# A decode layer on one core: all loads in one byte ring in transfer order, K a group ahead of V, and another order of the matmuls

## The chip, the cores and the metric

One core of one Trainium2 chip. The time is the device time of one execution in microseconds, the median of three or more executions. The span, which the profile shows, is about 2 us shorter than the time. TensorE is PE, its weight loads PEld, VectorE DVE, ScalarE ACT, and SP is the engine that issues all the DMA loads here. A load lands when its last byte is in SBUF.

## The reference

A pre-norm decode step for a batch of 2, one token each: attention over a cached window of 2048 positions, 32 heads of 192, then a GEGLU feed-forward layer (FFN). Everything is bf16.

```python
h  = x + attention(layernorm(x))          # q = ln(x) @ wq   [640 x 6144]
                                          # K, V: 32 heads x 2 batches x 2048 x 192, read once
                                          # o @ wo           [6144 x 640]
h2 = h + (gelu(ln(h) @ w_gate) * (ln(h) @ w_up)) @ w_down   # 640 -> 1536 -> 640
```

K and V are 100 MB of the 122 MB that must be read, so the floor is set by the loads.

## The kernel before

The 64 (head, batch) items are worked in 16 groups of four. Each K tile (768 KB) is turned by 12 PE transposes into three PSUM banks, and copied to SBUF by DVE and ACT. Scores, softmax and PV (the softmax weights times V) follow per group. A small scheduler in the program derives the semaphore waits from tokens that each operation reads or writes. Every engine executes its own list in order, so the order in which operations are emitted is the order in which PE runs them.

```python
KS = 6; VS = 8; WQS = 2; WOS = 3          # slots: K ring, V ring, wq ring, wo ring; wd has its own tile

def load_k(n): ... kring[:, n % KS, :]    # each load waits for the readers of its slot
# gate and up weights reuse the K ring: kflat[:, 0:7680], kflat[:, 7680:15360]

def transposes(n):                        # 3 banks in turn, 4 fp32-pair transposes each
    for c in range(3):
        ...
        if c == 2 or (c == 1 and n % 4 == 1):
            act(... activation(out=ktr[...], in_=bank, func=Copy))   # 5 of 12 copies a group
        else:
            dve(... tensor_copy(out=ktr[...], in_=bank))             # 7 of 12

for g in range(NG):                       # PE's order
    for j in range(4):
        transposes(4 * g + j)
        if j == 0 and g > 0: scores(g - 1)
        if j == 1 and g > 1: o_columns(g - 2)
        if j == 1 and g > 0: softmax(g - 1)
        if j == 2: oproj(g - 2); e_columns(g - 1); q_rows(g + 1)     # (guards cut)
        if j == 3: q_stationary(g + 1)
    if g > 0: pv(g - 1)
# ... last group, then the FFN loads are issued: gate and up in 10 pieces of 384 KB, wd in 3 of 640 KB
# down: uT is stationary (2 columns), wd moves: 24 matmuls of 320 columns
```

Between scores of a group and its softmax, and between softmax and what follows it, PE always has 12 transposes of the next group to do.

## Time and profile before

| | before |
|---|---|
| time, median | 315.41 us (314.92 to 315.9) |
| span | 313.6 us |
| bytes loaded | 122.3 MB |
| PE busy | 77% |
| last V complete | 289.4 us |
| last FFN weight complete | 308.3 us |

From the page of the kernel before, two of the rows that cut the span into 40 slices of 7.84 us: DMA is the busy tenths of the 16 DMA engines.

```profile
DMA  7999999999999999999999999999999999996891
GB/s 252 416 416 418 395 402 420 415 411 406 414 414 419 399 417 414 419 408 406 414 417 416 401 412 416 418 410 403 414 416 418 412 416 418 415 411 260 280 386 41
```

The DMA engines are full from the first microseconds to slice 36; the drop to 260 and 280 GB/s is the end, where the FFN weights wait for the K ring. The same page's chain of waits (what released what, followed back from the last instruction) says the same:

```profile
DMA 43%; PE 40%; ACT 8%; DVE 7%; issue 1%; SPq 1%; POOL 0%; ACTq 0%; POOLq 0%; DVEq 0%
```

PE waits for K, not the other way round. A stretch of that chain in order of time (its longest pieces; start, duration, what), from a group in which no load was waited for:

```profile
64.55 1.43 PE ops L530 x64
65.99 1.46 PE tps L404 x12
67.45 1.48 PE sps L485 x23
68.93 1.04 PE tps L404 x8
70.05 1.94 ACT ktr L417 x2
```

PV (ops), 12 transposes (tps), scores (sps), transposes: 12 transposes take 1.46 us. From PV at 64.55 to the next PV at 77.77, in the same view, is 13.2 us for a group.

The end, from the timeline (start, duration, engine, line, operation):

```profile
286.10 0.33 SPq L600 DMA_DIRECT2D kring<-in_B_w_gate_dram  x1
...
290.37 0.33 SPq L602 DMA_DIRECT2D kring<-in_B_w_up_dram  x1
...
306.20 5.28 PE L654 MATMUL tps<-wd_sb,uT 128*2 128x320 bf16 x24 [0.63 <-DVE uT L291]
...
312.04 0.28 SPq L660 DMA_DIRECT2D out_dram<-orow  x1
```

The weights of the FFN are asked for at 286.1 and 290.4, the down matmuls take 5.3 us, and the store goes out at 312.0, 1.6 us before the end of the span.

### The profile page before, as it was taken

The page shows a single profiled execution, that of the slowest core. Times are in us where ns is not written, and L with a number is a line of the kernel's source. Part 1 is how long each engine was busy: PE and PEld are TensorE (multiplying, and loading weights), DVE is VectorE, ACT ScalarE, POOL GpSimd, SP SyncE. Part 2 cuts the span into 40 slices and gives each one's busy share as a digit, 9 for nine tenths or more (in the row PEclk, how much of TensorE's full clock was granted, in tenths as well). Part 3 has the DMA queues.
Part 4 walks back from the last instruction along what each step waited for, and adds up shares of the span by engine and source line. Part 5 has one row for each costly group of instructions (what it writes and reads, how often), then busy time and mean ns, then how long its engine had stood idle before and what let it go on. Part 6 is the DMA issues. An engine that isn't in the chain of part 4 may idle for free.

```text
span 313.6 us, 6955 instructions
## 1 busy us (share of the span) xinstructions
PE 241.1 (77%) x3081; PEld 193.2 (62%) x3081; DVE 123.2 (39%) x340; ACT 124.6 (40%) x151; POOL 3.2 (1%) x9
## 2 busy tenths in 40 slices
PE   0597059898886896979679893979759895979786
PEld 0385047787675675757458773766557784767663
DVE  8145023455444253434424541443423453443120
ACT  1256014557544244445415650544514553542100
POOL 4000000000000000000000000000000000000000
PEclk9999657999999587788958996996958997987767
DMA  7999999999999999999999999999999999996891
GB/s 252 416 416 418 395 402 420 415 411 406 414 414 419 399 417 414 419 408 406 414 417 416 401 412 416 418 410 403 414 416 418 412 416 418 415 411 260 280 386 41
DMA packets 29045, 122.74 MB, mean 391 GB/s; under 512 B 2644, under 2 KB 9304, under 8 KB 29016
## 3 DMA queue, kind: packets, MB, share of 16 engines
q1 hardware_dynamic: 29016, 122.31, 97.1%
q8 instruction: 24, 0.39, 0.5%
q14 instruction: 5, 0.04, 0.0%
HBM read 122.29 MB, written 0.00 MB: 390 GB/s over the span
## 4 chain that ended last, share of the span: by engine, by line
DMA 43%; PE 40%; ACT 8%; DVE 7%; issue 1%; SPq 1%; POOL 0%; ACTq 0%; POOLq 0%; DVEq 0%
DMA kring<-in_A_k_cache_dram 43%; PE tps L404 18%; PE ops L530 5%; PE sps L485 5%; PE m L430 4%; ACT ktr L417 3%; ACT qrow L435 3%; PE tps L654 2%; PE m L515 2%; DVE ktr L421 2%; PE m L455 1%; DVE ering L514 1%; ACT eexp L498 1%; PE m L544 1%; PE m L507 1%
## 5 line engine op out<-in xcount | busy, mean ns | idle before, releaser
L404 PE MATMUL tps<-identf,kring 128*128 128x128 f32 x768 | 118.4, 315 | 45.8 <-DMA kring<-in_A_k_cache_dram 45.4
L404 PEld LDWEIGHTS tps<-identf,kring 128*128 128x128 f32 x768 | 102.1, 163 | 62.7 <-issue 61.7
L417 ACT ACTIVATE ktr<-tps 128x1024 bf16<-128x1024 bf16 x80 | 80.2, 1023 | 114.1 <-PE tps L404 113.9
L421 DVE COPY ktr<-tps 128x1024 bf16<-128x1024 bf16 x112 | 74.4, 687 | 96.4 <-PE tps L404 96.1
L435 ACT ACTIVATE qrow<-m 2x1536 bf16<-2x1536 f32 x16 | 23.0, 1439 | 30.0 <-PE m L430 30.0
L530 PE MATMUL ops<-vring,ering 128*32 128x192 bf16 x1024 | 25.3, 254 | 0.0
L485 PE MATMUL sps<-ktr,rq 128*32 128x512 bf16 x384 | 24.9, 392 | 0.0
L530 PEld LDWEIGHTS ops<-vring,ering 128*32 128x32 bf16 x1024 | 21.5, 99 | 0.6 <-issue 0.3
L430 PE MATMUL m<-wqring,xnT 128*2 128x384 bf16 x80 | 21.1, 408 | 0.9 <-DVE xnT L291 0.9
L544 PEld LDWEIGHTS m<-sel,osb 128*128 128x128 f32 x96 | 18.0, 260 | 1.4 <-ACT osb L539 1.0
L490 DVE TENSOR_REDUCE mx<-sps 128x1 f32<-128x512 f32 x16 | 11.1, 692 | 19.3 <-PE sps L485 19.3
L544 PE MATMUL m<-sel,osb 128*128 128x2 f32 x96 | 17.9, 302 | 0.6 <-ACT osb L539 0.6
L485 PEld LDWEIGHTS sps<-ktr,rq 128*32 128x32 bf16 x384 | 9.0, 95 | 10.2 <-issue 2.5
L515 PE MATMUL m<-zrhs,hm 128*128 128x2 f32 x32 | 7.6, 306 | 9.7 <-DVE ering L514 9.7
L539 ACT ACTIVATE osb<-ops 128x384 f32<-128x384 f32 x16 | 7.9, 492 | 17.0 <-PE ops L530 17.0
L515 PEld LDWEIGHTS m<-zrhs,hm 128*128 128x128 f32 x32 | 6.2, 241 | 13.2 <-DVE ering L514 13.2
L498 ACT ACTIVATE eexp<-sps,nm 128x512 bf16<-128x512 f32 x16 | 11.1, 692 | 2.6 <-DVE nm L496 2.6
L430 PEld LDWEIGHTS m<-wqring,xnT 128*2 128x2 bf16 x80 | 6.3, 94 | 7.5 <-issue 4.2
L514 DVE COPY ering<-m 128x64 bf16<-128x64 bf16 x16 | 6.9, 432 | 9.2 <-PE m L507 9.2
L291 DVE TENSOR_TENSOR rq<-m,mask 128x24 bf16<-128x24 f32 x64 | 7.2, 175 | 6.8 <-PE m L455 5.6
L556 PEld LDWEIGHTS hps<-ot,woring 128*128 128x128 bf16 x240 | 9.3, 104 | 1.0 <-DVE ot L291 0.3
L455 PEld LDWEIGHTS m<-identb,qrow 2*128 2x128 bf16 x192 | 5.9, 93 | 6.3 <-ACT qrow L435 5.0
(82 smaller groups left out, 99.4 us busy)
## 6 DMA issues: line engine op xcount, KB each, us to landing
kring<-in_A_k_cache_dram SPq DMA_DIRECT2D x64, 768.0 KB, 17.9
vring<-in_A_v_cache_dram SPq DMA_DIRECT2D x64, 768.0 KB, 17.1
wqring<-in_A_wq_dram SPq DMA_DIRECT2D x8, 960.0 KB, 17.8
woring<-in_A_wo_dram SPq DMA_DIRECT2D x16, 480.0 KB, 18.6
kring<-in_B_w_gate_dram SPq DMA_DIRECT2D x5, 384.0 KB, 5.9
kring<-in_B_w_up_dram SPq DMA_DIRECT2D x5, 384.0 KB, 6.9
wd_sb<-in_B_w_down_dram SPq DMA_DIRECT2D x3, 640.0 KB, 11.0
xrow<-in_A_x_dram SPq DMA_DIRECT2D x1, 2.5 KB
```

The costliest lines, as they stand in the source:

```text
L404: ins = e.transpose(tps[bi][:, 128 * u:128 * (u + 1)], kv[:, off:off + 128], identf[:, :])
L417: act(lambda e, c=c, kslot=kslot, bv=bv: e.activation(out=ktr[:, kslot, c, :], in_=bv[:, 0:1024], func=ACT.Copy), W=[("kt", kslot, c)], X= ...
L421: dve(lambda e, c=c, kslot=kslot, bv=bv: e.tensor_copy(ktr[:, kslot, c, :], bv[:, 0:1024]), W=[("kt", kslot, c)], X=[("t", bi)])
L430: ins = e.matmul(m1[0:2, 128:512], lhsT=xnT[:, c, :], rhs=wqring[:, J % WQS, c, off:off + 384], start=(c == 0), stop=(c == NC5 - 1))
L435: act(lambda e: e.activation(out=qrow[0:2, :, 0:rep, :], in_=m1[0:2, 128:512].rearrange("p (h d) -> p h d", h=2).unsqueeze(2).to_broadcast ...
L485: ins = e.matmul(sps[32 * j:32 * (j + 1), :], lhsT=rq[:, g % 2, j, k, :], rhs=r, start=(k == 0), stop=(k == 5), tile_position=(0, 32 * j))
L490: dve(lambda e: e.tensor_reduce(out=mx[:, :], in_=sps[:, :], axis=AX.X, op=ALU.max), W=["mx"], X=["s"])
L498: act(lambda e: e.activation(out=eexp[:, :], in_=sps[:, :], func=ACT.Exp, bias=nm[:, 0:1], scale=1.0, accum_out=zr[:, 0:1]), R=["nm"], W=[ ...
L514: dve(lambda e: e.tensor_copy(dst, src), W=[("er", g % 2)], X=["m2"])
L515: pe(lambda e: e.matmul(m2[:, 8:10], lhsT=hm[:, :], rhs=zrhs[:, :], start=True, stop=True), R=["hm", "zrhs"], X=["m2"])
L530: ins = e.matmul(ops_[32 * r:32 * (r + 1), 192 * hh:192 * (hh + 1)], lhsT=ering[:, g % 2, col:col + 32], rhs=vring[:, n % VS, DH * t:DH * ...
L544: ins = e.matmul(m1[:, 32 + 2 * kk:34 + 2 * kk], lhsT=osb[:, kk:384:3], rhs=sel[:, :], start=True, stop=True)
```

## The change

The intent: one ring of 110,592 bytes per partition holds K, V, wq, wo and the FFN weights, in the order in which they are transferred, so that no ring can run dry while another has room, and the FFN weights queue directly behind the last V. The ring is kept account of in granules of 768 bytes (GRAN): a load waits for the readers of every granule that it covers, so two pieces that share a granule wait for each other. K runs a group ahead of V. q is made for four groups at a time from one 1.9 MB load. Down has wd stationary and 2 moving columns, so that little is left after the last load.

```diff
-KS = 6
-VS = 8
-WQS = 2
-WOS = 3
+GRAN = 768
+RING = 18 * 6144
@@ loads: a queue, issued as soon as every older load on those bytes has been read
+        def pump():
+            while queue: ...
+                toks = [("ring", x) for x in range(off // GRAN, (off + nbytes + GRAN - 1) // GRAN)]
+                P.op("sp", lambda e, v=v, src=src: e.dma_start(v, src), W=toks + [("sem", i % NSEM)], ...)
+        load_k(0)
         load_wq(0)
+        load_k(1)
+        for g in range(NG):
+            if g > 0 and g + 1 < NG:
+                if (g + 1) % 4 == 0:
+                    load_wq((g + 1) // 4)
+                load_k(g + 1)
+            load_v(g)
+            load_wo(g)
+        load_ffn()
@@ PE's order
         for g in range(NG):
+            if g + 1 < NG:
+                for j in range(4):
+                    transposes(4 * (g + 1) + j)
+                    if (g + 1) % 4 == 0:
+                        q_rows(g + 1 + j)
+                q_stationary(g + 1)
+            pv(g, 0)
+            if g + 1 < NG:
+                scores(g + 1)
+            pv(g, 1)
+            pv(g, 2)
+            if g + 1 < NG:
+                softmax(g + 1)
+            pv(g, 3)
+            o_columns(g)
+            if g + 1 < NG:
+                e_columns(g + 1)
+            oproj(g)
@@ weights with contiguous rows per partition, so columns are read with a stride
-    lhsT=woring[:, g % WOS, kk, 128 * n5:128 * (n5 + 1)]
+    lhsT=wo[:, kk, c:D:NC5]                       # stride 5
-    lhsT=wv[:, c, 128 * f:128 * (f + 1)]          # gate, up
+    lhsT=wv[:, c, f:F:NF]                         # stride 12
@@ down
-    ins = e.matmul(tps[bank][0:2, 0:320], lhsT=uT[:, f, :], rhs=wd_sb[:, f, 320 * bank:320 * (bank + 1)], ...)
+    ins = e.matmul(m2[:, 2 * c:2 * c + 2], lhsT=wd[:, f, c:D:NC5], rhs=uT[:, 4 * i + f, :], ...)
@@ output: straight from the 128 x 2 x 5 result, 256 pieces of 10 bytes, instead of 2 rows
@@ cut: names of tokens, constants built after the first layernorm, q rows repeated 2 instead of 4 times
```

## The prediction

> **What bounds the kernel now.** The span is 313.6 us (time 315.8: 2.2 us lie outside it). The slice table shows the DMA row at 9 from 8 us to 274 us, at 395 to 420 GB/s; 122.3 MB moved. The chain of waits is 43% K loads. The body is bound by loads; PE (77% busy) waits for them. What is not stream is the end: the last V is complete at about 289.5 us, the gate/up loads wait for the K ring (issued 286.1 and, because the first up piece shares ring slots with the first gate piece, only after that landed, 290.4), 288-292 us moves 110 GB/s, wd streams until 307.5, down takes 5.3 us (306.2-311.5), output 1.6 us.
>
> The trace's landing records: each load lands on 16 DMA engines (Trainium skill, "DMA: Bandwidth & Descriptors", section on why a DMA increments its semaphore by 16: they finish independently, only the full count counts). The trace agrees: the first-to-last spread grows from 0.4 us at the start to 5.4 us at 289 us, in jumps of about 1 us that coincide with 16 KB instruction-fetch packets (1.1 us each). The fast engines finish V at 284, the slow one at 289.5. That lag survives the change.
>
> **What the change does.** Steady state: only packet size. Median packets: 1536 B (wq) 66 ns, 3072 B 121 ns, 6144 B 238 ns; wq in 3072 B rows saves about 1.5 us over the run. The K/V order is off the bound; PE work per group (my estimate 15 us, from the chain's 13 to 15 us stretches plus serial softmax waits) stays below the 17.4 us of loads per group, so DMA should not starve. Late constants and q for 4 groups: off the path.
>
> End: with FFN loads queued behind the last wo, the slow engine completes wo15 at about 288.0 us; wg, wu (1.97 MB each) and wd0 follow without gap: +11 us, 299. PV, output projection, layernorm, gate, GELU (10.7 us before, 295.5-306.2, with 1.4 us of residual matmuls removed) hide behind them. Down becomes 60 short matmuls (28 ns apart for the same form at gate/up); only the last 20, 0.6 us, follow the last load, instead of 5.3 us.
>
> But the wd pieces are 5120 B in 768 B granules, so neighbours share a granule, and the built program makes wd1's issue wait for wd0's semaphore and wd2's for wd1's. Before shows such an isolated load: the first up piece, 393 KB, took 3.0 us from issue to landing; 655 KB thus about 3.7 us (estimate). wd2 lands near 306.3 instead of 302. Then matmuls, an add, a scattered output store: 2.7 us. Span 309.
>
> **Predicted: 311.0 us (-1.5%), 80% range 307.0 to 314.5. Faster by over 2%: 0.28; within 2%: 0.68; slower: 0.04.**
>
> **Right if:** DMA still about 415 GB/s; gate/up issued long before landing; wd1 and wd2 waiting for a load in the SP queue's waits (two dips in the last 10 us); under 3.5 us after wd2's landing.
>
> **Wrong if:** the wd waits cost under 1 us each (307); strided weight loads (every 5th or 12th bf16) are slow: stride 2 shows no penalty (92 ns), every third f32 takes 261 ns against 190 contiguous; at 100 ns apart, 317; PE falls behind after q for 4 groups and stalls the ring (+2 to 5); the slowest engine's fetch lag changes by some us.

## The result, and the profile after

| | before | after |
|---|---|---|
| time, median | 315.41 us | 325.52 us (323.86 to 327.21) |
| ratio | | 1.032 (1.026 to 1.038) |
| last V complete | 289.4 us | 289.0 us |
| last PV done | 295.5 us | 303.0 us |
| last FFN weight complete | 308.3 us | 309.5 us |

A ratio is the mean time of one kernel's fast runs over that of the other's in the same rounds, so it is not quite the ratio of the medians quoted.

The change made it 10 us slower. The slices of the page after (8.1 us each now; PEclk is the TensorE clock that the throttle granted, in tenths of full speed):

```profile
PEclk9997797979799786979799897979796898979555
DMA  7999999999999999999999999999999999998310
GB/s 274 416 416 414 419 417 416 410 409 419 413 391 329 422 413 419 411 412 414 414 386 413 418 414 417 407 418 414 413 368 419 419 414 415 414 427 371 104 66 0
```

The loads still run at 416 GB/s and nearly end with slice 37, three slices before the end; three dips (329, 386, 368) have appeared. And the chain of waits no longer holds a load:

```profile
PE 59%; ACT 24%; DVE 12%; issue 3%; POOL 0%; ACTq 0%; POOLq 0%
```

PE, fed by ACT and DVE, has become the bound. One whole group of that chain, in order of time (its longest pieces; it answers to the stretch shown of before):

```profile
260.60 0.70 DVE mx L521
261.33 0.24 DVE mrhs L316
261.61 0.40 PE m L525 x2
262.03 0.17 DVE nm L527
262.29 0.78 ACT eexp L529 x2
263.07 0.39 ACT osb L570
263.50 1.21 PE m L575 x6
264.71 0.26 PE m L538 x4
264.99 0.45 DVE ering L545
265.48 0.38 PE m L546 x2
265.86 0.58 PE hps L589 x15
266.45 3.92 PE tps L433 x20
270.39 1.95 ACT ktr L448 x2
272.39 0.67 PE tps L433 x4
273.08 1.03 ACT ktr L448
274.16 0.67 PE tps L433 x4
274.85 1.03 ACT ktr L448
276.02 1.56 PE sps L516 x24
277.60 0.70 DVE mx L521
```

In it mx is the maximum of each row of scores, m L525 and nm bring the rows of an item together, eexp is the exponential, osb and m L575 turn the attention output of the group before, m L538 and ering turn the exponentials, and hps is the output projection. From one maximum (mx) to the next is 17.0 us. The first 5.85 us are the softmax block: each step waits for the one before it on another engine, and PE has only PV matmuls (32, then 16) to do beside them. Then come the 48 transposes in one burst, 9.6 us to the start of the scores. The first 20 take 3.92 us, 196 ns each, against 122 ns before (1.46 us for 12). The rest alternate with ACT's copies, since three PSUM banks are all that the kernel gives them and every bank must be emptied first. Then scores, 1.6 us. In the three of the fifteen periods that make q for four, the period is 20.3 us instead of 17.0. The mean over groups 2 to 16 (fourteen periods) is 17.8 us, and the loads of a group take 17.4 (9.25 tiles' worth on average, with wo and wq, at 1.88 us a tile from landing to landing).

The end of the kernel, from the timeline:

```profile
309.14 3.72 PE L637 MATMUL sps<-hnT,ring 128*128 128x2 bf16 x60 [0.80 <-DVE hnT L320]
...
316.69 2.56 PE L660 MATMUL m<-uT,ring 128*128 128x2 bf16 x60 [0.28 <-DVE uT L320]
...
319.49 0.41 SPq L668 DMA_DIRECT2D out_dram<-yT  x1
```

All weights are there at 309.5, but gate has only started. The 10.2 us of span divide as follows. PV of the last group ends 7.5 us later (303.0 against 295.5). From there to gate it is 0.6 us shorter; gate to the GELU product 7.5 us instead of 3.9 (+3.6); from there to the issue of the store 2.9 instead of 5.9 (-3.0); issue of the store to the end 4.3 instead of 1.6 (+2.7).

### The profile page after: what moved, and what is told of

It reads as the page before. It is cut to its first block, busy times and chain, and to the rows that moved or that the text cites. A ratio compares the mean times of both kernels' runs of the same rounds, so it can differ in the third digit from the quotient of the medians.

```text
span 323.8 us, 6976 instructions
## 1 busy us (share of the span) xinstructions
PE 255.5 (79%) x3105; PEld 203.3 (63%) x3105; DVE 126.1 (39%) x340; ACT 112.8 (35%) x150; POOL 3.2 (1%) x9
## 4 chain that ended last, share of the span: by engine, by line
PE 59%; ACT 24%; DVE 12%; issue 3%; POOL 0%; ACTq 0%; POOLq 0%
PE tps L433 27%; ACT ktr L448 16%; PE sps L516 8%; PE m L575 6%; PE m L461 4%; ACT eexp L529 4%; DVE mx L521 3%; PE hps L589 3%; DVE ering L545 2%; PE m L546 2%; PE m L525 2%; ACT osb L570 2%; ACT qrow L466 2%; PE m L538 1%; DVE mrhs L316 1%
## 5 line engine op out<-in xcount | busy, mean ns | idle before, releaser
L433 PE MATMUL tps<-identf,ring 128*128 128x128 f32 x768 | 124.3, 326 | 11.8 <-ACT ktr L448 8.9
L433 PEld LDWEIGHTS tps<-identf,ring 128*128 128x128 f32 x768 | 109.2, 170 | 24.9 <-ACT ktr L448 17.8
L575 PE MATMUL m<-sel,osb 128*128 128x2 f32 x96 | 19.9, 324 | 16.1 <-ACT osb L570 16.1
L575 PEld LDWEIGHTS m<-sel,osb 128*128 128x128 f32 x96 | 18.6, 270 | 19.9 <-ACT osb L570 19.9
L561 PE MATMUL ops<-ring,ering 128*32 128x192 bf16 x1024 | 30.7, 253 | 0.0
L561 PEld LDWEIGHTS ops<-ring,ering 128*32 128x32 bf16 x1024 | 21.8, 98 | 3.8
L516 PEld LDWEIGHTS sps<-ktr,rq 128*32 128x32 bf16 x384 | 9.7, 97 | 16.5 <-DVE rq L320 8.6
L461 PE MATMUL m<-ring,xnT 128*2 128x384 bf16 x80 | 17.7, 357 | 2.7 <-ACT qrow L466 2.7
L466 ACT ACTIVATE qrow<-m 2x768 bf16<-2x768 f32 x16 | 12.6, 790 | 4.9 <-PE m L461 4.9
L461 PEld LDWEIGHTS m<-ring,xnT 128*2 128x2 bf16 x80 | 5.7, 87 | 11.4 <-ACT qrow L466 4.4
L589 PEld LDWEIGHTS hps<-ot,ring 128*128 128x128 bf16 x240 | 12.1, 134 | 0.3 <-DVE ot L320 0.3
L525 PEld LDWEIGHTS m<-mrhs,pm 128*128 128x128 f32 x32 | 4.8, 188 | 11.3 <-DVE mrhs L316 11.3
L589 PE MATMUL hps<-ot,ring 128*128 128x2 bf16 x240 | 11.6, 177 | 0.3 <-DVE ot L320 0.3
```

The lines of the kernel that those rows point to most:

```text
L433: ins = e.transpose(tps[bi][:, 128 * u:128 * (u + 1)], kv[:, off:off + 128], identf[:, :])
L461: ins = e.matmul(m1[0:2, 128:512], lhsT=xnT[:, c, :], rhs=wq[:, c, off:off + 384], start=(c == 0), stop=(c == NC5 - 1))
L466: act(lambda e: e.activation(out=qrow[0:2, g % QS, :, 0:rep, :], in_=m1[0:2, 128:512].rearrange("p (h d) -> p h d", h=2).unsqueeze(2).to_b ...
L516: ins = e.matmul(sps[32 * j:32 * (j + 1), :], lhsT=rq[:, g % 2, j, k, :], rhs=r, start=(k == 0), stop=(k == 5), tile_position=(0, 32 * j))
L561: ins = e.matmul(ops_[32 * r:32 * (r + 1), 192 * hh:192 * (hh + 1)], lhsT=ering[:, g % 2, col:col + 32], rhs=vv[:, DH * t:DH * (t + 1)], s ...
L575: ins = e.matmul(m1[:, 32 + 2 * kk:34 + 2 * kk], lhsT=osb[:, kk:384:3], rhs=sel[:, :], start=True, stop=True)
```

## The experiments

Theory A: the new PE order is the loss. Before, transposes lay between the dependent steps of the softmax; now the steps are waited for one after the other and the transposes come in a burst, so a group costs PE 17 us or more. Theory B: the ring is the loss. It frees in order and leaves gaps at its end, so loads come late (the dips). Two smaller causes are separate: the strided weight loads of the FFN, and the waits between wd pieces on which the prediction put 4.4 us.

### 1. The changed kernel with the PE order of before (e1_interleave)

```diff
-        (the order shown in the change)
+        for g in range(NG):
+            for j in range(4):
+                transposes(4 * g + j)
+                if g % 4 == 0 and g > 0: q_rows(g + j)      # g == 0: all four after j == 3
+                if j == 0 and g > 0: scores(g - 1)
+                if j == 1 and g > 1: o_columns(g - 2)
+                if j == 1 and g > 0: softmax(g - 1)
+                if j == 2: oproj(g - 2); e_columns(g - 1)   # guards cut
+                if j == 3: q_stationary(g)
+            if g > 0: pv(g - 1, 0..3)
+        # cut: the last group, as in the kernel before
```

> The changed kernel with the PE order of the kernel before (K transposes of one group between scores, softmax and projection of the last), loads and FFN as changed. Theory A (the serial PE order is the loss: a group takes PE 17.0 us, 20.3 with q, against 17.4 us of loads): the chain is led by loads again, the dips to 270-350 GB/s in the body go, PV of the last group ends before 293 us instead of 303, time 311 to 317. Rival B (the byte ring, with its in-order freeing and wrap gaps, starves the loads): the dips stay and the time stays above 320. Then, with PE on time, the two waits of wd pieces should show as dips near the end.

Measured: 314.75 us, ratio to before 0.997 (0.994 to 1.000). Of the three dips one small one is left (376 GB/s). Where no load is waited for, a group takes 12.0 us from maximum to maximum instead of 17.0, and the last wo is complete at 287.75 us (the prediction had 288.0). Theory B alone cannot stand: ring, loads and FFN are all those of the changed kernel, and 10.8 us are gone.

The chain of this run ends with what the prediction had expected of the changed kernel:

```profile
298.46 3.93 DMA ring<-in_B_w_down_dram
...
302.47 3.87 DMA ring<-in_B_w_down_dram
...
306.39 1.77 PE m L667 x40
```

Two wd loads, each issued only when the one before has landed, 3.95 us from landing to landing for 1.6 us worth of bytes. They had been estimated at 3.7. And one detail nobody had seen: 40 matmuls come after the last load, not 20, because readers of a shared granule wait for its last writer too.

### 2. The kernel before with the PE order of the change (e2_before_order)

The reverse: rings, loads and FFN of before, K transposed a group ahead, then the serial order. q_rows stays one group at a time.

```diff
+        k_group(0); q_stationary(0); scores(0); softmax(0); e_columns(0)   # k_group: transposes, K loads, q_rows
+        for g in range(NG):
+            k_group(g + 1); q_stationary(g + 1)                            # guards cut
+            pv(g, 0); scores(g + 1); pv(g, 1); pv(g, 2); softmax(g + 1); pv(g, 3)
+            o_columns(g); e_columns(g + 1); oproj(g)
```

> The kernel before (its own rings, loads and FFN) with only the PE order of the changed kernel, K a group ahead. Theory A: PE becomes the bound, group period 17.5 to 18.5 us, time 320 to 328. Rival B (the ring is the loss, the order harmless): within 1% of before, 313 to 318.

Measured: 337.29 us, ratio 1.068 (1.065 to 1.072). The order alone makes the old kernel 22 us slower. The direction is theory A's, the size is beyond what was expected: after the first, periods are 17.9 to 19.2 us, because in this kernel every group also has its own q rows, whose copy takes ACT 1.44 us (0.79 in the changed kernel, where rows are repeated half as often) inside the burst that already waits for ACT. The changed kernel's cheaper q copy is thus a gain that its order hides. What q for four groups is worth by itself, no run shows: the shorter copy comes from the halved repetition.

### 3. Gate and up read contiguously (e3_contig)

```diff
-                        ins = e.matmul(..., lhsT=wv[:, c, f:F:NF], ...)
+                        ins = e.matmul(..., lhsT=wv[:, c, 128 * f:128 * (f + 1)], ...)
-            wd = B_w_down.rearrange("(p f) n -> p f n", f=NF)
+            wd = B_w_down.rearrange("(f p) n -> p f n", p=128)
```

> The changed kernel with the gate and up weights read contiguously (wd loaded in 1280 B rows to match), the rest as changed. If the stride of 12 is what makes a gate matmul 62 ns instead of 28: gate and up take 1.7 to 1.9 us each instead of 3.7 and 3.6, and, since PE is last, the time falls by 3 to 4 us to about 322. If the half clock is the cause instead: no change, 325.

Measured: 319.7 us, 5.8 us under the changed kernel's 325.52 (different rounds; ratios to before 1.013 and 1.032). The timeline of this run:

```profile
307.52 1.76 PE L637 MATMUL sps<-hnT,ring 128*128 128x2 bf16 x60 [0.79 <-DVE hnT L320]
```

Gate (this line) and up (1.74 us) take half as long as in the changed kernel (3.72 and 3.69) at the same granted clock (0.50 in both kernels). So the stride costs 62 ns a weight load against 28 to 29. That is 3.6 us of the 6.3 between the two profiled runs. The rest: gate began 1.6 us earlier, and the store was 1.1 us shorter; neither is explained by the edit. Runs of the changed kernel differ by 3.4 us among themselves, so the first may be chance.

The Trainium skill's page "SBUF — State Buffer" (the cacheline note) says that accesses that leave the 16-byte line each time pay a penalty, without a number for weight loads. The traces agree for steps of 24 bytes and supply numbers: stride of 4 bytes, 30 ns (12 q columns in 0.36 us before, on 2 partitions only and at a granted clock of 1.00); at 0.50, 10 bytes, 43 ns (60 down matmuls in 2.56 us); 24 bytes, 62 ns; contiguous, 28 ns. The note's figure for how far one can stride for free, 8 bf16 elements, they do not bear out: the step of 10 bytes is 5 elements and already costs.

### 4. Granules of 256 bytes (e4_gran256)

```diff
-GRAN = 768
+GRAN = 256
```

> The changed kernel with ring granules of 256 B instead of 768 B, so that wd pieces share none and do not wait for each other. The prediction put 4.4 us on these waits. Theory A (PE is 10 us late at the end): wd lands some 4 to 7 us earlier and the time moves by less than 1 us (324 to 326). If the waits cost what was predicted: about 321.

Measured: 325.14 us, ratio 1.029 (1.024 to 1.034). wd is complete at 302.6 us instead of 309.5, seven microseconds earlier, and nothing moves: PE reaches down at 315.8. The waits on which the prediction built its arithmetic existed and were hidden.

### 5. One more copy on DVE (e6_evac)

```diff
-                if c == 2 or (c == 1 and n % 4 == 1):
+                if c == 2:
```

> The changed kernel with its serial PE order kept, and one of the five K copies that ACT does per group moved to DVE (4 on ACT, 8 on DVE). Theory A, where the burst of 48 transposes waits for ACT's copies: the group's period falls from 17.0 to about 16.0 us, below the 17.4 us of loads, the dips shrink and the time falls to 314 to 320. If ACT's copies are not what stretches the burst: 325, no change.

Measured: 324.0 us, ratio 1.027 (1.019 to 1.036), its runs overlapping those of the changed kernel. A miss. PE's wait for ACT before transposes falls from 8.9 to 3.6 us in all, but the periods without q, after the first, are 16.5 us in five groups and 17.2 to 17.4 in six. In the six, part of a stretch of half clock fell into the softmax block (mean grant there 0.74 to 0.78 instead of 1.00), which then took 6.2 to 6.3 us instead of 5.7. So there is a second brake, the clock. The last wo was complete at 287.8 us here, as early as in experiment 1, and PE was still late.

### 6. Useless matmuls that keep PE busy in the softmax block (e9_warm)

```diff
+        def warm(n):                       # n matmuls of 128 x 88 columns into unused columns of m1
+            ...
             softmax(g + 1)                 # warm(6) before it
             pv(g, 3)
+            warm(18)
             o_columns(g)                   # and warm(8) inside e_columns, before the sum
```

> The changed kernel, its order kept, with 32 useless matmuls of 88 columns per group put where PE waits in the softmax block (before the max matmul, before the output columns, before the sum matmul). If the half clock after that block is what stretches the transposes (196 ns instead of 122 for the first 20 of 48 in a group): they run at 122, the period falls from 17.0 to 15.3 to 16 us although PE does more, loads lead again and the time falls to 314 to 319. If the clock is only a symptom: the period stays at 17 or grows, 325 to 328.

Measured: 318.32 us, ratio 1.009 (1.007 to 1.012); 506 more matmuls and 7 us faster than the changed kernel. In the groups that took 15.6 or 15.7 us, the chain reads:

```profile
209.02 2.55 PE tps L433 x20
```

The first 20 transposes take 2.55 us instead of 3.92. Of the eleven periods without q after the first, three came down to 15.6 or 15.7, three are 16.8 to 16.9, and five stayed at 17.0. (The first is 15.8, but it was 15.1 in the changed kernel.) The granted clock tells them apart. First the changed kernel around the start of a burst, then this run around a burst that stayed slow (stretch, its length, PE busy and instructions, granted clock, DMA share, GB/s):

```profile
263.06:266.47 3.41, 2.44 (x29) 1.00 1.03 421
266.47:269.88 3.41, 3.41 (x18) 0.50 1.03 419
269.88:273.29 3.41, 2.95 (x24) 1.00 0.99 407
```

```profile
242.07:245.48 3.41, 3.37 (x41) 1.00 1.02 409
245.48:248.90 3.42, 3.42 (x19) 0.50 1.02 418
```

In the three fast groups the grant stays at 1.00 through the burst, in the other eight its first 4 us are granted 0.57 to 0.59. Program and order are the same in all of them, so the clock is a cause, not only a symptom, and it is worth 1.4 us a group. That idle PE in the block is what lowers it is not shown: here PE was busy for 3.37 of the 3.41 us before the grant fell, and why three groups escaped is open. The Trainium skill's "TensorE: Matmul & The Clock Gate" (Part 1) describes a clock that is half by default and full only after a stretch of PE activity; the traces here agree that it is either half or full and comes back after 3.41 us of transposes, but a busy PE was not enough to keep it.

### 7. Two of four tiles transposed inside the softmax block (e10_two_early)

```diff
                 for j in range(4):
-                    transposes(4 * (g + 1) + j)
+                    if g == 0 or j > 1: transposes(4 * (g + 1) + j)
             pv(g, 3)
+            transposes(4 * (g + 2))          # guards cut
             o_columns(g)
             e_columns(g + 1)
+            transposes(4 * (g + 2) + 1)
             oproj(g)
```

> The changed kernel with two of the four K tiles of the next group but one transposed inside the softmax block (before the output columns and before the output projection), the rest of the order, loads and FFN as changed. Theory A (waits of the softmax block plus a burst that waits for copies): the period falls to about 15.5 us, under the 17.4 of loads, time 313 to 317, close to the fully interleaved 314.75. If only the complete order of before helps: above 320.

Measured: 314.92 us, ratio 0.998 (0.995 to 1.000). Groups that wait for no load take 13.6 us. The chain leads from loads again (38% DMA, 27% of it K), and the transposes in the block run at 122 ns, with a grant of 1.00 through block and burst (249.93 to 260.70):

```profile
250.94 0.38 PE m L525 x2
...
251.77 1.46 PE tps L433 x12
253.23 0.94 PE m L575 x6
```

Compare the same place of the changed kernel: from L525 at 261.61 to L575 at 263.50 PE had only 16 PV matmuls. Two moves undo the loss in the body; the complete order of before is not needed.

### 8. The parts put together (e5b_inter_gran, e5_all, e8_rowout)

Experiment 1 with 256-byte granules:

> The PE order of before with 256 B granules: the two waits of wd pieces, hidden where PE was late, should now be worth what they cost in the interleaved run (3.9 us each for 1.6 us of transfer). wd2 complete at about 302 instead of 306.7, 20 matmuls behind it instead of 40, time 309.5 to 311.5 (4 to 5 us under the interleaved run's 314.75). If it stays at 314 or more, something else paces the end.

Measured: 309.87 us, ratio 0.980 (0.975 to 0.986), 4.9 us under experiment 1. With PE on time the same one-line edit that did nothing in experiment 4 is worth what its waits cost. Last wd complete at 301.5 us.

The same with gate and up contiguous:

> The same, and gate and up read contiguously. The strided reads end at about 301 us in the run without it, before wd2 lands (302), so they should be hidden: 0 to 1 us less, 309 to 311. A gain of 3 us or more would say that the FFN matmuls are still on the path.

Measured: 307.94 us, ratio 0.9745 (0.969 to 0.980). 1.9 us less, where at most 1 was expected. The timelines show the difference: without it down begins at 301.05, 0.5 us before the last load lands, and its 60 matmuls end at 303.6; with it 20 remain after the last load, and the store is issued 0.7 us earlier. The store itself takes 2.9 us instead of 4.5 to the end of the span. The two kernels with contiguous gate and up and this store have 2.9 and 3.2 us, the seven strided ones 4.3 to 4.7, with the same store; why is open.

The same with the output turned into two rows on PE, copied by DVE and ACT and stored in 1280-byte pieces:

> The same, and the output turned into 2 rows on PE and stored in 1280 B pieces, instead of 256 pieces of 10 B. The store took 4.3 us from issue to the end of the span in the changed kernel against 1.6 us before; five matmuls and a split copy add about 1.3 us. Net 1 to 1.7 us less than the run before it: 307.5 to 309.5.

Measured: 308.37 us, no gain. The store does take 1.6 us, but the way to it from the last landing is 3.2 us instead of 1.3: DVE's copy of 2 x 384 with a stride of 5 in the output took 1.21 us, where the contiguous 2 x 320 copy of the kernel before took 0.48. The Trainium skill's "DMA: Bandwidth & Descriptors" (Specifications) asks for 512 bytes or more per piece; the trace agrees that 10-byte pieces are slow (2.9 to 4.7 us against 1.6), but avoiding them costs as much here.

The version of e5_all beats both kernels: 2.5% under before (by the interval of the ratio, 2.0 to 3.1%), 5.4% under the changed one (307.94 against 325.52, medians of different rounds).

## Why the prediction was wrong

- **The step that failed:** "PE work per group (my estimate 15 us ...) stays below the 17.4 us of loads per group, so DMA should not starve." Measured: 17.0 us, 20.3 with q, 17.8 in the mean. The estimate added the serial waits to durations of an interleaved kernel. It left out that a burst of transposes on three banks waits for its copies, and that after the serial block the clock is at half for the first 3.4 us of the burst. The burst takes 9.6 us where four tiles take 5.8 at 1.46 each. Of these 3.8 us the clock is about 1.4 (an estimate: the full-clock groups of experiment 6 against the others), and the remaining 2.4 would be waits for copies, the last one before the scores included. Experiments 1, 2 and 7 show that the order is the cause, 6 that the clock has a share; 5 that ACT's copies alone are not enough.
- **What followed from it:** the estimate left 2.4 us of slack per group; there were -0.4. And 17.4 was too generous a yardstick, since at the first maximum the loads have already been running for some 30 us. Where they lead (experiment 1), first and last maximum are at 29.4 and 279.8 us, 16.7 a period; in the changed kernel at 30.4 and 294.6, 17.6 a period. Fifteen periods that are 0.9 us longer are 14 of the 15.6 us by which the last PV ends later than in experiment 1 (303.0 against 287.4). Experiment 6 shows the same: 17.3 a period, under 17.4, PE never waits for a load, and the last PV ends at 295.8.
- **"The wd pieces ... 3.7 us", "wd2 lands near 306":** right as a mechanism (3.95 each, 306.3 in experiment 1), and off the path in the kernel as changed (experiment 4). A correct cost was placed on a path that another one had taken over.
- **"Strided weight loads are slow"** was named as a way to be wrong, with 100 ns; it is 62 at a stride of 12. In the changed kernel it costs 3.6 us; with everything else repaired, 0.7 us of matmul time.
- **The output:** "matmuls, an add, a scattered output store: 2.7 us" measured 6.3 us in experiment 1: 40 matmuls at 44 ns (1.8), the add 0.2, the store 4.3.
- **"That lag survives the change"** (slowest of the 16 DMA engines 5.4 us behind): only while the stream does not pause. At the end of attention it was 2.6 us in the changed kernel, with its three dips, and 5.3 in e5_all; in experiment 1 it fell from 5.1 to 3.1 in the one dip. The full count of a load's semaphore is what is waited for, as the Trainium skill's "DMA: Bandwidth & Descriptors" says (Why a DMA increments its semaphore by 16 and not by 1).
- **wq in 3072-byte rows, about 1.5 us:** consistent; the last byte of attention was complete 1.7 us earlier in e5_all (287.75 against 289.4).

Open: what lowers the clock after the serial block, and the two lengths of the store.

## What to carry to other kernels

When loads are the bound, PE's idle time looks free, and an order of its work that only "adds a few waits" seems harmless; compute PE's period for the new order, step by step through every engine that each step waits for, and at the clock that a trace of such an order shows, before calling it slack. Independent work placed between dependent steps did three things at once here: it filled the wait, it spread the demand for copies, and the clock stayed up (experiment 7). And when a cost is found, ask what else must be on time for it to show: the same one-line repair was worth 0 us in one surrounding and 4.9 in the next.

## What the Trainium skill lacked or had wrong

- "SBUF — State Buffer", cacheline note: no number for weight loads. Here 128 bf16 columns: 28 ns contiguous, 30 at a stride of 4 bytes (2 partitions), 43 at 10, 62 at 24.
- "TensorE: Matmul & The Clock Gate", Part 4 (PE-mode transpose), says that the full clock does not engage for transposes. Here 12 transposes took 1.46 us in stretches granted 1.00 and up to 2.79 us in stretches granted 0.50, and the grant came back to 1.00 after 3.41 us in which PE ran only transposes (266.47 to 269.88 in the changed kernel). The page does not say whether matmuls of few columns count as activity: those of gate and up, 2 columns each, kept PE busy from 309.2 to 316.4 us in the changed kernel, and the grant stayed at 0.50.
- No page has a number for what instruction fetches cost the loads that share the DMA engines with them. In the kernel before there were 24 packets of 16 KB, about 1.1 us each, and the slowest of the 16 engines was 5.4 us behind the first by the last V. Three of the four larger steps of this lag (0.6 to 1.5 us) came 2.2 to 3.5 us after a fetch; that the fetches make it is likely and not shown.
- "DMA: Bandwidth & Descriptors", fixed cost (Anatomy of one DMA): its fit is for loads issued from GpSimd. A load of 655 KB issued from SP with nothing in flight took 3.95 us from the landing before it to its own.
